# Gated linear attention with a rational MLP in fp32: the last 128 tokens leave as one piece, under another table of steps

## The chip, the cores and the metric

The kernel runs on one core of one Trainium2 chip. The metric is the time of one execution on the device, in microseconds (us); lower is better. The page of the profile and the trace come from one profiled execution, which has a time of its own beside those of the timed runs.

## What is computed

The inputs are q, k, v and alpha of 4 x 8 heads, 768 positions, 48 channels, and the weights of an MLP. Everything is fp32.

```python
state = zeros(B, H, D, D)                     # B=4, H=8, S=768, D=48
for t in range(S):
    state = alpha[:, :, t, :, None] * state + einsum('bhd,bhe->bhde', k[:, :, t], v[:, :, t])
    y[:, :, t] = einsum('bhd,bhde->bhe', q[:, :, t], state)
x = y.transpose(0, 2, 1, 3).reshape(B * S, H * D)   # 3072 x 384
h = x @ w_in                                        # 384 -> 2048
P = a[0] + a[1] * h + a[2] * h**2 + a[3] * h**3
Q = 1 + abs(b[0]) * abs(h) + abs(b[1]) * h**2
out = (P / (Q + 1e-6)) @ w_out                      # 2048 -> 384
```

## The kernel before

**Steps and their order.** The whole kernel is a list of 2813 steps, each a small function for one engine, added to a `Plan` with the steps that must come before it. `Plan.run` (L44) writes them out in the order of a table of numbers, `ORDER` (L72 to L139): each number is the index of a step, and its top bit says that the step's alternate engine is taken, where it has one. The engines' queues run in order, so the table settles what stands behind what on each engine, and which engine does a step that two can do. For a step on DVE that is marked `lock`, the next POOL step in the table waits until it has ended (L60 to L66).

**Attention.** 24 chunks of 128 tokens, named by g. Per chunk alpha is transposed on DVE (L454), k and q are transposed (L459), running products are made by a scan (L462) and a reciprocal (L471); k and q are scaled by them on POOL or DVE (L483, L486), the scores are copied by ACT (L525) and masked by POOL (L531), PE forms the products (L504, L537, L568, L586), and POOL and ACT carry totals and the state (L545, L547, L556, DVE L597). The output of a chunk, a piece of x, is copied out of PSUM by ACT and split into a high and a low part, the low part on DVE (L633, or for the first four chunks L626 on DVE or POOL).

**MLP.** 96 units of 128 x 512 elements of h, named by u: 16 slices of the 2048 columns for each super-block of 512 tokens; the first 8 are smaller, plain fp32 ones. A unit's input product on PE (L695, 9 matmuls of high and low parts) goes into one of three banks, so unit u waits until unit u - 3 has left its bank. Then ACT takes the absolute value (L750) and a linear part (L753), ACT or POOL makes the start of Q (L759 on ACT, L757 on POOL), POOL multiplies (L762), DVE makes P (L773, L777, L787), ACT adds and takes the reciprocal (L780, L783), DVE finishes (L790, L796: the step `g`), ACT rounds the result to its high part (L799: `gh`), POOL or DVE makes the low part (L803: `gl`), and PE multiplies with w_out (L714; L708 in the last super-block, where tokens stand on partitions).

**Weights.** They arrive as doubles and are put together to fp32 from their words: scaled (L270 on ACT or L272 on POOL: `join_scale`), shifted (L278 on DVE), their sign (L282) and the joining itself (L298 on DVE: `join`); the high part is rounded on ACT (L313) and the low part made on POOL (L318).

**A guard** reads alpha again in the second half (L849 on ACT), sums up (L859 on DVE, L862 on PE) and leaves a number (L865) that every engine loads at the end.

**The end.** The last super-block's output stands in four banks, one for each tile tt of 128 tokens x 384 columns. After the last unit's low part, PE adds the last products tile by tile (L723; `og` is the high part's, `ot` the low part's). Then `last_done` (L738) copies a tile out of PSUM, on ACT by an activation (L741), on DVE by a copy (L743), and `last_store` (L745) sends it to DRAM (L747). Tiles 0 and 2 are copied by DVE, tile 1 by ACT, and SP's queue issues their stores. Tile 3 is cut into two halves of 192 columns: the first is copied by DVE and stored by SP, the second copied by ACT and stored by ACT's own queue. The plan's code for this is at L1122 to L1133.

## Time and profile before

| | us |
|---|---|
| median of 3 runs | 529.98 |
| lowest, highest | 529.82, 531.18 |
| the profiled execution's own time | 531.47 |
| its span, first to last instruction | 529.4 |
| PE busy (share of the span) | 501.9 (95%) |
| DVE busy | 494.2 (93%) |
| ACT busy | 459.1 (87%) |
| POOL busy | 423.5 (80%) |

The profiled execution takes 2.07 us more than its span, which lie outside the instructions. The mean granted clock of TensorE is 0.988. A busy share is an average over stages: the first quarter of the span holds the attention's start and the weights, the middle runs both parts side by side, and the end holds the MLP alone. Units, chunks and tiles are told apart by the order of their instructions on an engine, since a row of the trace names only the line.

### The profile page before, as it was taken

To read this page: it belongs to the slowest core of one execution; us is meant where nothing else is said; L and a number is where in the kernel's file an instruction comes from. 1 tells how busy PE (TensorE), PEld (TensorE's weight loads), DVE (VectorE), ACT (ScalarE), POOL (GpSimd) and SP (SyncE) were. 2 spreads that over 40 slices of the span, in tenths; PEclk is the share of its full clock that TensorE was granted. 3 is DMA by queue.
4 is the path that set the end of the run, shared out by engine and by line. 5 is a ranking of instruction groups with operands and counts; after the bars stand their busy time and mean duration, and the time that the engine had idled before them with its cause. 6 is when DMAs were issued, how large, how long until landed. Compare 5 with 4: busy or idle time off the path is not lost.

```text
span 529.4 us, 13659 instructions
## 1 busy us (share of the span) xinstructions
PE 501.9 (95%) x5082; PEld 411.9 (78%) x5082; DVE 494.2 (93%) x773; ACT 459.1 (87%) x805; POOL 423.5 (80%) x421
## 2 busy tenths in 40 slices
PE   7865988987999999999999999999999999999996
PEld 7864866865778778778787887878888878888996
DVE  4899899999999999999999999999999999898885
ACT  4988999999999888888898898898898897997892
POOL 3447667999999998989898888889888887876782
PEclk9997998999999999999999999999999999999998
DMA  9899684465565454554546445351646201023001
GB/s 262 248 250 268 155 197 88 106 152 132 127 144 117 89 105 100 97 99 94 119 86 116 111 91 100 83 113 32 120 83 130 47 2 41 0 61 59 2 2 63
DMA packets 145656, 56.81 MB, mean 107 GB/s; under 512 B 133424, under 2 KB 138160, under 8 KB 145584
## 3 DMA queue, kind: packets, MB, share of 16 engines
q1 hardware_dynamic: 145440, 55.78, 46.4%
q8 instruction: 41, 0.67, 0.6%
q14 instruction: 31, 0.25, 0.2%
q10 hardware_dynamic: 144, 0.10, 0.1%
HBM read 47.98 MB, written 4.72 MB: 100 GB/s over the span
## 4 chain that ended last, share of the span: by engine, by line
PE 81%; ACT 6%; DVE 4%; SPq 4%; DMA 3%; issue 1%; POOL 1%; DVEq 0%; POOLq 0%
PE ps L695 34%; PE ps L714 28%; PE ps L708 6%; PE ps L586 4%; PE ps L681 2%; PE ps L504 2%; PE ps L568 2%; SPq L408 2%; PE ps L537 1%; DMA wi_words<-in_moe_w_in_dram 1%; ACT wo_words L282 1%; DMA wo_words<-in_moe_w_out_dram 1%; PE ps L668 1%; SPq L448 1%; SPq L401 1%
## 5 line engine op out<-in xcount | busy, mean ns | idle before, releaser
L695 PE MATMUL ps<-x,wi 128*128 128x512 f32 x792 | 204.4, 398 | 1.7 <-DVE t L796 1.7
L695 PEld LDWEIGHTS ps<-x,wi 128*128 128x128 f32 x792 | 146.5, 188 | 34.7 <-DVE t L796 2.7
L714 PE MATMUL ps<-gh_gl,wo 128*128 128x512 f32 x648 | 170.2, 399 | 0.2 <-ACT gh_gl L799 0.2
L714 PEld LDWEIGHTS ps<-gh_gl,wo 128*128 128x128 f32 x648 | 119.1, 188 | 27.2 <-ACT gh_gl L799 0.6
L762 POOL TENSOR_TENSOR qm<-qm,ah 128x512 f32<-128x512 f32 x96 | 124.2, 1294 | 14.8 <-ACT qm L759 5.9
L803 POOL TENSOR_TENSOR gh_gl<-t,gh_gl 128x512 fp32r<-128x512 f32 x83 | 108.6, 1309 | 16.3 <-ACT gh_gl L799 11.8
L753 ACT ACTIVATE t<-ps,coef 128x512 f32<-128x512 f32 x96 | 74.7, 778 | 6.9 <-PE ps L695 4.8
L787 DVE SCALAR_TENSOR_TENSOR t<-t,coef,ps 128x512 f32<-128x512 f32 x96 | 70.7, 737 | 6.5 <-ACT ps L783 5.1
L780 ACT ACTIVATE ps<-qm,one_eps 128x512 f32<-128x512 f32 x96 | 66.4, 691 | 11.5 <-DVE t L777 6.1
L750 ACT ACTIVATE ah<-ps 128x512 f32<-128x512 f32 x96 | 57.0, 594 | 20.6 <-PE ps L695 19.4
L777 DVE SCALAR_TENSOR_TENSOR t<-t,coef,ps 128x512 f32<-128x512 f32 x96 | 70.9, 739 | 1.0
L757 POOL TENSOR_SCALAR qm<-ah,bab 128x512 f32<-128x512 f32 x61 | 47.9, 786 | 28.6 <-ACT ah L750 16.8
L773 DVE TENSOR_TENSOR t<-t,ps 128x512 f32<-128x512 f32 x96 | 64.9, 677 | 4.6 <-ACT t L753 2.9
L796 DVE SCALAR_TENSOR_TENSOR t<-ps,t 128x512 f32<-128x512 f32 x96 | 65.6, 683 | 1.1
L790 DVE SCALAR_TENSOR_TENSOR ps<-qm,ps 128x512 f32<-128x512 f32 x96 | 65.9, 687 | 0.2
L783 ACT ACTIVATE ps<-ps 128x512 f32<-128x512 f32 x96 | 56.1, 585 | 2.0
L799 ACT ACTIVATE gh_gl<-t 128x512 fp32r<-128x512 f32 x88 | 55.1, 627 | 3.0 <-DVE t L796 2.8
L531 POOL TENSOR_SCALAR_AFFINE_SELECT tqk<-tqk 64x512 f32<-64x512 f32 x48 | 33.1, 690 | 13.9 <-ACT tqk L525 7.6
L486 POOL TENSOR_TENSOR tqk<-tqk,fp 128x512 f32<-128x512 f32 x22 | 28.9, 1312 | 8.9 <-DVE wi_words L298 7.7
L462 DVE TENSOR_TENSOR_SCAN tg<-ta,ps 128x528 f32<-128x528 f32 x24 | 29.7, 1242 | 6.6 <-ACT ta L444 6.5
L586 PEld LDWEIGHTS ps<-tqk,sv 128*32 128x32 f32 x1536 | 23.4, 112 | 15.1 <-POOL tqk L531 7.1
L483 POOL TENSOR_TENSOR tqk<-tqk,tg 128x512 f32<-128x512 f32 x23 | 30.4, 1322 | 5.6 <-ACT tqk L444 5.3
(112 smaller groups left out, 728.8 us busy)
## 6 DMA issues: line engine op xcount, KB each, us to landing
...
sv<-in_v_dram SPq DMA_DIRECT2D x48, 96.0 KB, 2.6
...
```

What stands on the lines that cost most here:

```text
L695: nc.tensor.matmul(h_of(u), w(key)[:, kt * FU + f % FU, :], x[:, kt, xp, :], start=(n == 0), stop=(n == len(todo) - 1),)
L714: nc.tensor.matmul(bank(O_BANKS[dt]), w(("o", f // FU))[:, f % FU, dt * P : (dt + 1) * P], g, start=(f == 0 and first_w), stop=(f == NF - ...
L750: nc.scalar.activation(buf(s, "ah", u), h_of(u), AF.Abs)
L753: nc.scalar.activation(buf(s, "t1", u), h_of(u), AF.Identity, bias=a2, scale=a3)
L762: nc.gpsimd.tensor_tensor(buf(s, "qm", u), buf(s, "qm", u), buf(s, "ah", u), op=ALU.mult)
L773: nc.vector.tensor_tensor(t, t, h_of(u), op=ALU.mult)
L777: nc.vector.scalar_tensor_tensor(t, t, a1, h_of(u), op0=ALU.add, op1=ALU.mult)
L780: nc.scalar.activation(h_of(u), buf(s, "qm", u), AF.Abs_reciprocal_sqrt, bias=one_eps)
L787: nc.vector.scalar_tensor_tensor(t, t, a0, h_of(u), op0=ALU.add, op1=ALU.mult)
L790: nc.vector.scalar_tensor_tensor(h_of(u), buf(s, "qm", u), 1.0 + 1e-6, h_of(u), op0=ALU.add, op1=ALU.mult)
L796: nc.vector.scalar_tensor_tensor(t, h_of(u), 2.0, t, op0=ALU.subtract, op1=ALU.mult, reverse0=True)
L803: eng.tensor_tensor(buf(s, "gl", u).rearrange("p a b -> p (a b)"), buf(s, "t1", u), gh, op=ALU.subtract)
```

## The change

Tile 3 is no longer cut. ACT copies all of its 128 x 384 elements and ACT's queue stores them; the other three tiles are as they were. That leaves 2811 steps instead of 2813: one copy and one store fewer.

```diff
-    def last_done(eng, tt, c0, c1):
-        o, x = parts[:, tt * DM + c0 : tt * DM + c1], bank(T_BANKS[tt], DM)[:, c0:c1]
+    def last_done(eng, tt):
+        o = parts[:, tt * DM : (tt + 1) * DM]
         if eng is nc.scalar:
-            eng.activation(o, x, AF.Copy)
+            eng.activation(o, bank(T_BANKS[tt], DM), AF.Copy)
         else:
-            eng.tensor_copy(o, x)
+            eng.tensor_copy(o, bank(T_BANKS[tt], DM))
-    def last_store(eng, tt, c0, c1):
+    def last_store(eng, tt):
         r = (NSUP - 1) * SUP + tt * P
-        eng.dma_start(out[r : r + P, c0:c1], parts[:, tt * DM + c0 : tt * DM + c1])
+        eng.dma_start(out[r : r + P, :], parts[:, tt * DM : (tt + 1) * DM])
...
-                    cut = DM // 2 if tt == PER - 1 else DM
-                    for c0 in range(0, DM, cut):
-                        part = (m, tt, c0) if c0 else (m, tt)
-                        act = c0 > 0 or tt == 1
-                        add(("wd", *part), "ACT" if act else "DVE", 0.5 if cut == DM else 0.33, last_done, (nc.scalar if act else nc.vector, tt, c0, c0 + cut), [("ot", tt)] + old, due=at + 3)
-                        add(("ws", *part), "ACT" if c0 else "SP", DMA, last_store, (nc.scalar if c0 else nc.sync, tt, c0, c0 + cut), [("wd", *part)], kb=0.55 * cut / DM)
+                    act, own = tt % 2, tt == PER - 1
+                    add(("wd", m, tt), "ACT" if act else "DVE", 0.5, last_done, (nc.scalar if act else nc.vector, tt), [("ot", tt)] + old, due=at + 3)
+                    add(("ws", m, tt), "ACT" if own else "SP", DMA, last_store, (nc.scalar if own else nc.sync, tt), [("wd", m, tt)], kb=0.55)
```

The table `ORDER` is replaced by another of 2811 numbers (two of its lines are enough to see that nothing can be read from them):

```diff
-    'c-jTQ1E3u`3;@t3X_~gPZQHhO+qS*k?fK2NZQHhO+xFi-XN*!Rx^gOtLN!)RQeLr&t;VUzDykZ<jGCubs3|I%TBxR~`D&t',
+    'c-jrsgQ6X}5&+Q5WG0iOwr$(CZQHin-5#IXwr$(CZQH(mZ~ep?qm=T>DORYWsOV~v8mD5ZXey?Pt&AG4mZ`C7o|>#ysJLp',
```

Forty-six steps go to the other one of their two engines. The start of Q goes to ACT 43 times (35 before) and to POOL 53 times (61), though at the start it goes to POOL for units 0, 1 and 10 and to ACT for units 2 and 9. The low part `gl` goes to DVE 8 times (5 before), six of them among the last ten units, where it was one. One `join_scale`, the fourth of w_in, moves from ACT to POOL (L272). The low part of x for chunk 1 moves from DVE to POOL (L626). One scaling of q, three score copies and five copies of totals change sides as well. The rest of the table keeps its broad sequence, with steps exchanged over a few places.

**POOL, early.** The stretch between the masking of chunk 1 (L531 on tqk_89) and that of chunk 2 (L531 on tqk_90). Before:

```order
L531 AFFINE_SELECT tqk_89<-tqk_89 64x8x64 x2
L62 MEMSET floor_s 128x1
L483 TENSOR_TENSOR tqk_90<-tqk_90,tg_86 128x512
L486 TENSOR_TENSOR tqk_88<-tqk_88,fp_85 128x512
L762 TENSOR_TENSOR qm_103<-qm_103,ah_98 128x512
L483 TENSOR_TENSOR tqk_88<-tqk_88,tg_87 128x512
L556 TENSOR_TENSOR sv_91<-st_s,tots_94 48x4x48
L556 TENSOR_TENSOR sv_91<-st_s,tg_86 48x4x48
L356 MEMSET raw_odd_82 128x48
L531 AFFINE_SELECT tqk_90<-tqk_90 64x8x64 x2
```

After, on the same engine at the same place:

```order
L483 TENSOR_TENSOR tqk_90<-tqk_90,tg_86 128x512
L626 TENSOR_TENSOR x_358<-x_whole,x_358 128x3x128
L757 TENSOR_SCALAR qm_103<-ah_98,bab 128x512
L272 TENSOR_SCALAR parts<-wi_words 128x768
L556 TENSOR_TENSOR sv_91<-st_s,tots_94 48x4x48
L556 TENSOR_TENSOR sv_91<-st_s,tg_86 48x4x48
L762 TENSOR_TENSOR qm_103<-qm_103,ah_98 128x512
L757 TENSOR_SCALAR qm_104<-ah_99,bab 128x512
L762 TENSOR_TENSOR qm_104<-qm_104,ah_99 128x512
L483 TENSOR_TENSOR tqk_88<-tqk_88,tg_87 128x512
L531 AFFINE_SELECT tqk_90<-tqk_90 64x8x64
```

The scaling of q for chunk 3 (L486 on tqk_88) now comes behind the masking of chunk 2; the low part of x for chunk 1, the start of Q for units 0 and 1, the scaling of a piece of w_in and the product of unit 1 have moved ahead of it.

**DVE, around the end of unit 12** (its L796 is the one on t_100; the L298 on parts and wo_words is the joining of the eighth piece of w_out). Before:

```order
L633 TENSOR_TENSOR x_1106<-ps,x_1106 128x3x128
L462 SCALAR_TENSOR_TENSOR tg_86<-ta_83,ps 128x528
L298 SCALAR_TENSOR_TENSOR parts<-parts,wo_words 128x768
L787 SCALAR_TENSOR_TENSOR t_100<-t_100,coef,ps 128x512
L773 TENSOR_TENSOR t_101<-t_101,ps 128x512
L790 SCALAR_TENSOR_TENSOR ps<-qm_103,ps 128x512
L777 SCALAR_TENSOR_TENSOR t_101<-t_101,coef,ps 128x512
L796 SCALAR_TENSOR_TENSOR t_100<-ps,t_100 128x512
L459 STREAM_TRANSPOSE tqk_90<-raw_qk_81 128x16x2x32
```

After:

```order
L462 SCALAR_TENSOR_TENSOR tg_86<-ta_83,ps 128x528
L796 SCALAR_TENSOR_TENSOR t_102<-ps,t_102 128x512
L787 SCALAR_TENSOR_TENSOR t_100<-t_100,coef,ps 128x512
L471 RECIPROCAL ta_83<-tg_86 128x4
L773 TENSOR_TENSOR t_101<-t_101,ps 128x512
L790 SCALAR_TENSOR_TENSOR ps<-qm_103,ps 128x512
L777 SCALAR_TENSOR_TENSOR t_101<-t_101,coef,ps 128x512
L796 SCALAR_TENSOR_TENSOR t_100<-ps,t_100 128x512
L298 SCALAR_TENSOR_TENSOR parts<-parts,wo_words 128x768
L459 STREAM_TRANSPOSE tqk_90<-raw_qk_81 128x16x2x32
```

The joining has moved from ahead of unit 12's last operations to behind them, and a reciprocal of 128 x 4 has come in.

**ACT, at the end** (t_102 is the last unit's). Before:

```order
L799 ACTIVATE gh_gl<-t_101 128x512
L799 ACTIVATE gh_gl<-t_102 128x512
L741 ACTIVATE parts<-ps 128x384
L741 ACTIVATE parts<-ps 128x192
L747 DMA out_dram<-parts 128x192
```

After:

```order
L799 ACTIVATE gh_gl<-t_101 128x512
L799 ACTIVATE gh_gl<-t_102 128x512
L849 ACTIVATE wr_78,beyond<-wr_78,lim 128x512
L741 ACTIVATE parts<-ps 128x384 x2
L747 DMA out_dram<-parts 128x384
```

The half copy and the half store have become whole ones, and the guard's last activation stands between the last unit's rounding and the first of ACT's copies. On DVE the copy of 128 x 192 is gone and the guard's sum (L859) has come in ahead of the two copies that stay; on SP the store of 128 x 192 is gone. On PE the last products of a tile (`og`, then `ot`) now follow each other tile by tile, where before `og` of the next tile came ahead of `ot` of the one before.

## Rows read from the trace of the kernel before

**Rows 1.** Busy time by stretch: us, then busy us (x instructions) by engine, PEclk, DMA, GB/s.

```profile
20.00:40.00 20.00, 15.03 (x287) 13.63 (x285) 18.54 (x27) 17.88 (x33) 8.93 (x10) 1.00 0.95 280
120.00:140.00 20.00, 17.28 (x193) 13.09 (x192) 19.82 (x31) 18.54 (x33) 19.16 (x18) 1.00 0.54 124
140.00:440.00 300.00, 300.00 (x3056) 239.85 (x3056) 293.57 (x466) 264.61 (x488) 266.09 (x257) 1.00 0.46 96
480.00:522.00 42.00, 42.00 (x216) 38.51 (x215) 36.30 (x56) 33.50 (x60) 31.08 (x28) 1.00 0.05 8
```

**Rows 2.** Waits of PE from 100 to 140 us: us in total, times, longest.

```profile
PE ps L568 <- ACT tqk L525: 1.6, 1, 1.6
PE ps L537 <- DVE x L633: 1.6, 1, 1.6
PE ps L695 <- DVE t L796: 1.1, 1, 1.1
```

**Rows 3.** Timeline of the end: start, us, engine, line, operation, idle before and its releaser.

```profile
521.96 0.69 DVE L803 TENSOR_TENSOR gh_gl<-t,gh_gl 128x512 fp32r<-128x512 f32 x1 [0.81 <-ACT gh_gl L799]
522.33 2.26 PE L723 MATMUL ps<-wo,gh_gl 128*128 128x384 f32 x12
523.93 0.49 ACT L741 ACTIVATE parts<-ps 128x384 f32<-128x384 f32 x1 [2.06 <-PE ps L723]
...
524.11 0.89 DVE L743 COPY parts<-ps 128x384 f32<-128x384 f32 x2
525.02 0.33 ACT L741 ACTIVATE parts<-ps 128x192 f32<-128x192 f32 x1 [0.60 <-DVE parts L743]
525.39 0.39 ACTq L747 DMA_DIRECT2D out_dram<-parts  x1
...
524.91 0.90 SPq L747 DMA_DIRECT2D out_dram<-parts  x2
```

**Rows 4.** DMA issues from 515 to 530 us: tiles, queue, count, KB each, us to landing.

```profile
out_dram<-parts SPq DMA_DIRECT2D x3, 192.0 KB, 2.0
out_dram<-parts ACTq DMA_DIRECT2D x1, 96.0 KB, 2.0
out_dram<-parts SPq DMA_DIRECT2D x1, 96.0 KB, 2.2
```

**Rows 5.** Timeline of DVE and of POOL from 122 to 130 us.

```profile
123.89 2.46 DVE L298 SCALAR_TENSOR_TENSOR parts<-parts,wo_words 128x768 uint32<-128x768 uint32 x1
...
128.78 0.68 DVE L796 SCALAR_TENSOR_TENSOR t<-ps,t 128x512 f32<-128x512 f32 x1
...
123.69 1.84 POOL L318 TENSOR_TENSOR wi<-wr,wi 128x768 fp32r<-128x768 f32 x1
```

**Rows 6.** DVE and ACT by line and tiles: count, busy us, mean ns, idle before.

```profile
L626 DVE TENSOR_TENSOR x<-x_whole,x 128x384 fp32r<-128x384 f32 x2 | 1.1, 550 | 0.4 <-ACT x L622 0.4
...
L298 DVE SCALAR_TENSOR_TENSOR wo_words<-wr,wo_words 128x768 uint32<-128x768 uint32 x2 | 1.9, 952 | 0.0
...
L759 ACT ACTIVATE qm<-ah,bab 128x512 f32<-128x512 f32 x35 | 28.5, 814 | 0.6 <-DVE ps L790 0.5
```

**Rows 7.** Timeline of DVE and of PE around 153 us (the L796 is unit 17's, the L695 unit 20's).

```profile
152.61 0.69 DVE L796 SCALAR_TENSOR_TENSOR t<-ps,t 128x512 f32<-128x512 f32 x1
...
153.71 0.73 PE L695 MATMUL ps<-x,wi 128*128 128x512 f32 x2
```

**Rows 8.** Timeline of POOL from 20 to 46 us.

```profile
36.01 1.27 POOL L486 TENSOR_TENSOR tqk<-tqk,fp 128x512 f32<-128x512 f32 x1 [7.67 <-DVE wi_words L298]
```

**Rows 9.** POOL by line and tiles, whole span.

```profile
L757 POOL TENSOR_SCALAR qm<-ah,bab 128x512 f32<-128x512 f32 x61 | 47.9, 786 | 28.6 <-ACT ah L750 16.8 <-DVE gh_gl L803 2.8 <-ACT t L753 2.1
...
L318 POOL TENSOR_TENSOR wi<-wr,wi 128x768 fp32r<-128x768 f32 x6 | 11.1, 1851 | 0.2
...
L626 POOL TENSOR_TENSOR x<-x_whole,x 128x384 fp32r<-128x384 f32 x2 | 2.0, 1016 | 1.7 <-DVE wo_words L278 1.7
```

**Rows 10.** Busy time by stretch, 100 to 180 us, columns as in rows 1.

```profile
100.00:180.00 80.00, 75.42 (x798) 58.98 (x797) 78.95 (x124) 75.67 (x128) 77.40 (x67) 1.00 0.54 125
```

More of the change, by code (lines that the diff above doesn't have):

```diff
@@ L133 @@
[L133 to L136 removed]
+    'c-jrsgQ6X}5&+Q5WG0iOwr$(CZQHin-5#IXwr$(CZQH(mZ~ep?qm=T>DORYWsOV~v8mD5ZXey?Pt&AG4mZ`C7o|>#ysJLp',
+    'mile5eg=)T<swS$aYPL$NR;meVhFYW+sKsivTB4Q))&;s@ckGFvdSG4^U#(K{RDbM+q<Z5<wMK1F(^Mbqi%HdVbz03)Wz{',
@@ new lines @@
+    'B?K=s3{YOOk@2I3aIUTxLe)MhmR)2Z}oyV7bD&QjZg&ZrE5-D(idRD*G^8iEN`MzvK9!{L};z0eaz1@M6Su7j|E8i701P@',
+    'JohsV!<G?okKTF11qyV<^^D+w~!}U+vH@bw2e&ztXRD2=3Hxg31Nv;RzLn6Y-=vtlsKy{Hc?xYpSUFrO&G0K@nJ0{n7hWi',
+    'oj?rua2m3SWq2T?{tO07`&+7>#_J(A5+=X2W^$1NX)LrV?}jd<p_M#N7a8irK+z!>3V7s4p0r$KmA!>QD5|BB{T&sDT<*c',
+    '<9q}vu8=%A+NGn?1+`l@QP)*56^-K29(_rbP@1OVLp2SfP<*Pcrek!9K@U_z)k)37SvUuCs;~N+o{cl`o+_zgQUY3ljZ`c',
+    'mI;ZC1Q<W%q5!O%(F*YTnB$SxeU~6?>-B5dVQmUqIs>Xq)s+oGOlF=YlQ{7Q_RdQlVLHl%CN=J{>3zd@6QwDmbGE>Ij!72',
@@ new lines @@
+    '`AqCC`GrJ^hpm)7D{wO_YTc_}NUru>wKx~R4)8)c``REXNB$Eu}zrEaOk*iJ3MeDqR1Q9acg)hcjXm7xN`pH&WOua;p>>a',
+    '4!0vQ(IAQ90_MDpEmOhr?A@RfK-1j)A2(P`y^=gS)AsG(;`O-l`bYre3NN^-;y?t*SsJs4}g<FDe)1rYiJRt-`)4pjuLhs',
+    '!IQ<-)a|rQt#DztV?xhB@R{9Xf;NI-S|&6pnBAbO40_bPQO%r`lE&gN>M{<O(WD#^<BMFaiA@EIG`I5z(I}BhI&(bYDXVb',
+    'A8JfBs0sB`9cUx|RZVH6+JqYVQcdbd{i!20qyB+`v>7doQVu?<0i<9ncA{+<Ogk`yniD}3*omRknYQ2{>OzC51?|D@*p<S',
+    'A_aZ|g6{O<A5Sm6YU?|0eFcOHQL%JIcBLjzZR7k8MXgZCi?vxU`s~!{^_F;VJNn>a~j-}`@oO%RiQZE`u$>9Jd35=jnl>i',
@@ L137 @@
+    'bg!G4He;ivl<ex;x3hx%oak$#pR<Cpu<ezqU$SNYX`oSWm<__cnVpX=B8d49fM;Me<&enaFYztwN^i~UZ&%YXAf{ARz!Z}',
+    '&U=ZokLx_51vOf589rzx@9IB$L{y',
 ]
```

113 lines of the change are left out of this document (50 added, 63 removed).

## The prediction

> **What bounds the kernel now.** I read the busy time by stretch first [rows 1]. From 140 to 440 us PE is busy for all of its 300.00 us, and from 480 to 522 us for all of its 42.00. No idle PE time can be taken out of these stretches. What a new order can save lies ahead of about 130 us and behind the last product; it can also open gaps where there are none, since DVE is busy 293.57 of the 300 us and so has little to spare.
>
> Next I read PE's waits from 100 to 140 us [rows 2]: three are left there, 1.6, 1.6 and 1.1 us, behind ACT's score copy, DVE's low part of x and DVE's last operation on unit 12. In the stretch from 120 to 140 us DVE is busy 19.82 of 20 us [rows 1], so the way to shorten these waits is less DVE work in front of them. The end I read from the timeline [rows 3]: PE's last 12 products run from 522.33 for 2.26, to 524.59, and everything behind that is copy, store and the loading of the guard's number, 529.4 - 524.6 = 4.8 us to the end of the span.
>
> **The end, part by part.** Before: DVE copies tiles 0 and 2, then its half of tile 3, and ends at 524.11 + 0.89 = 525.00. ACT's half starts only at 525.02, 0.60 us of waiting that the trace puts down to DVE's copy, takes 0.33 and lets ACT's store be issued at 525.39 [rows 3]. SP issues its last two stores from 524.91 for 0.90 us, so the very last is issued from about 524.91 + 0.45 = 525.4. It lands 2.2 us later, at 527.6; ACT's lands 2.0 later, at 527.4 [rows 4].
>
> After: ACT's whole copy costs 0.49 (tile 1's row) and depends on PE alone. It starts at about 524.64, a little after 524.59, ends at 525.13 and lets the store be issued about 0.04 later, as 525.35 to 525.39 was [rows 3], at 525.17. The store is 192 KB now, as three of SP's were, and those landed in 2.0 us, no later than the 96 KB ones [rows 4]: 527.2. The last landing moves from 527.6 to 527.2, **-0.4**. SP has one issue less (-0.45) and can go on to the end sooner by that. The two bounds are -0.5, where SP's own sequence sets the end, and 0, where the loading of the guard's number sets it: that load is issued by all engines behind the guard's result, which isn't earlier. The trace has no row that says which of the two; I take -0.4, since landing and issue both move by that much.
>
> The guard's activation behind the last rounding on ACT and its sum on DVE lie beside PE's twelve last products, 2.26 us long [rows 3], so I cost them at nothing. ACT has 2.06 us idle there. If that cover were gone, the first copy would be late by under 1 us, and it isn't the last one. The tile-by-tile order on PE costs no product more. It brings `ot` of tile 0 forward by one `og`, two of the twelve products or 2 x 0.19 = 0.38 us. That one needs the last low part, which DVE ends at 521.96 + 0.69 = 522.65; its new place is 522.33 + 0.38 = 522.71. So the slack there falls from about 0.4 to almost nothing; a DVE that is late by 0.5 us would then cost 0.5. DVE gets low parts of six among the last ten units and loses two just ahead of them, but has 42.00 - 36.30 = 5.7 us idle from 480 on [rows 1]. I cost this at 0, with +0.5 as its other end.
>
> **The start, part by part.** Two changes on DVE matter for the last waits. The low part of x for chunk 1, 0.55 us on DVE, goes to POOL, where it takes 1.02 [rows 6, 9]. And the joining of the eighth piece of w_out moves from ahead of unit 12's end to behind it; it took 2.46 us [rows 5], where the others of its kind take 0.95 [rows 6].
>
> How much of this reaches the end is read at the first place where PE is gap-free afterwards. Unit 20's input product starts at 153.71 and needs unit 17's L796, which ends at 152.61 + 0.69 = 153.30: a slack of 0.41 [rows 7]. PE is one packed sequence from there on, so the end moves by what this product moves. What stands on DVE ahead of unit 17 differs by the 0.55 alone (the joining is behind unit 12 now, but still ahead of unit 17). If DVE stays as full as it is, unit 20 can start at 153.30 - 0.55 = 152.75, which is **-0.96**; the waits of 1.6, 1.6 and 1.1 then shrink by this sum between them, the 0.41 of slack being given up. If the joining also takes its usual 0.95 in its new place, another 2.46 - 0.95 = 1.51 go, and the sum is -2.47. The other end is 0: where POOL or ACT takes DVE's place as the engine that these waits come from. I take -0.96, since the joining's new place has POOL beside it as full as its old one, 77.40 of 80 us [rows 10].
>
> The row on the joining deserves a second look. It started at 123.89, 0.2 us after a POOL subtraction of two tiles that ran from 123.69 to 125.53; taken from that end, the joining lasted 126.35 - 125.53 = 0.82, about its usual length [rows 5, 6]. The Trainium skill has a rule for it (SBUF — State Buffer, "SBUF: two separate sides"): a GpSimd instruction and a DVE instruction with two SBUF inputs share a port pair as an exclusive lock, and whoever starts first keeps the other out for its whole instruction. The trace agrees. By that rule the sum is -0.96 if the joining's new place finds such a POOL instruction just begun again, and -2.47 if it finds POOL at rest; nothing in the order of the two engines' queues settles which.
>
> On POOL the early stretch gets four instructions more ahead of chunk 2's masking: the low part of x, 1.02; two starts of Q, 2 x 0.79 = 1.57; and a scaling of 128 x 768 [rows 9]. POOL shows no row for this scaling; its bounds are 0.79 x 768/512 = 1.18 (the same kind of operation on 512 columns) and 1.85 (POOL's other operation on 768 columns, with two inputs) [rows 9]. I take 1.2, by the kind. The sum is 3.8, up to 4.4. What hides it: POOL waited 7.67 us at 36.01 with its scaling of q behind a joining on DVE [rows 8], and was busy 8.93 of 20 us [rows 1]. That wait is now behind chunk 2's masking, and the new work stands in its place. So I cost it at nothing. With the cover gone, up to 3.8 us of it come later. ACT loses one scaling and three starts of Q early, gets two back, and gets eight more in all, 0.81 us each [rows 6]. Most of them lie in the gap-free stretch, where ACT is busy 264.61 of 300 us [rows 1]. I cost them at nothing: 35 us of idle ACT time stand against 8 x 0.81 = 6.5.
>
> **The sum.** -0.96 - 0.4 = -1.36, rounded to -1.3 for the rounding of the ends. The profiled execution took 531.47 us, 2.07 of them outside the span of 529.4; it would take 530.2, with a span of 528.1. It stands 1.5 above the median of the runs, 529.98, so the median becomes 528.7.
>
> **Rivals.** (1) **Only the end changes**: POOL or ACT holds PE at the last waits instead of DVE, and -0.4 remains: 529.6. For it speaks POOL's share there, 77.40 of 80 us. Against it: two of the three waits name DVE [rows 2]. (2) **Faster**: the joining is free of POOL in its new place, -2.47 - 0.5: 527.0. For it speaks that most joinings took 0.95; against it, that unit 15 and the next units have waits of their own, which become the bound once those go. (3) **Slower**: POOL's new early work doesn't fit into the 7.67 us, because the instructions in it wait for their inputs in another order than they stand in. Then up to 3.8 us of work is pushed down POOL's queue, PE's waits for maskings and scalings ahead of 140 us grow, and the start brings a loss instead of -0.96. Between 100 and 180 us POOL has 80 - 77.40 = 2.6 us to catch up [rows 10]. If it can use all of that, 3.8 - 2.6 = 1.2 stay, and with -0.4 of the end the time is 529.98 + 0.8 = 530.8; if it can use none of it, 529.98 + 3.8 - 0.4 = 533.4; the middle is 532.1. It decides from the point where POOL reaches 100 us more than 2.6 us later than before. For it speaks how full POOL is there; against it, that 7.67 is twice 3.8. (4) **The change doesn't do what it says**: ACT's last copy waits for something other than PE, or the whole piece lands later than two halves; then the end gives 0 and the start alone -0.96: 529.0.
>
> **How the numbers follow.** The forecast, within 0.7 of 528.7, gets 0.45; rival 1 gets 0.17, rival 2 gets 0.15, rival 3 gets 0.18, rival 4 gets 0.05. A measurement can tell about 0.3% from no change, 1.6 us: faster means below 528.4, slower above 531.6. Below 528.4 lie rival 2 and nearly half of the forecast's own case, 0.15 + 0.2 = 0.35; above 531.6 lies most of rival 3, 0.15; the rest, 0.5, is within. The range leaves out the upper part of rival 3, some 0.16, and little of rival 2, whose 527.0 is the sum of the lower bounds: 526.9 to 531.2.
>
> **What would show it.** In the trace after: ACT's second copy at L741 with 128 x 384 elements, idle before it put down to PE, its store issued about 0.5 us behind the last product, and 4.4 us from the last product to the end of the span where it was 4.8. PE's waits between 100 and 140 us that sum to about 3.4 us instead of 4.4, the joining behind unit 12's L796, and unit 20's input product about 1 us earlier. No wait of PE after 155 us. Wrong would be: POOL's masking as the releaser of PE's waits ahead of 130 us, POOL's wait of 7.67 us still there with the new work behind it, a PE wait for DVE's L803 at the end, or a joining near 2.5 us again, which leaves the start at no more than -0.96.

## The result, and the profile after

The changed kernel took 532.98 us (median of 16 runs, 529.98 to 536.55), the kernel before 529.92 beside it (16 runs, 528.25 to 532.85): a ratio of 1.0062, 95% interval 1.0035 to 1.0088. It is slower by 0.6%, where 528.7 was forecast, and lies above the range of 526.9 to 531.2. The runs of the changed kernel come in two groups: eight of the 16 at 529.98 to 532.17, eight at 533.79 to 536.55. The profiled execution is one of the second: 536.37 us, its span 534.6.

**The end** did what was forecast. This is its timeline (start, us, engine, line, operation, idle before and its releaser), and below it the DMA issues from 515 to 536 us:

```profile
528.01 2.27 PE L723 MATMUL ps<-wo,gh_gl 128*128 128x384 f32 x12
...
529.33 1.39 SPq L747 DMA_DIRECT2D out_dram<-parts  x3
...
530.32 0.49 ACT L741 ACTIVATE parts<-ps 128x384 f32<-128x384 f32 x1 [0.56 <-PE ps L723]
...
530.84 0.38 ACTq L747 DMA_DIRECT2D out_dram<-parts  x1
```

```profile
out_dram<-parts SPq DMA_DIRECT2D x3, 192.0 KB, 1.9
out_dram<-parts ACTq DMA_DIRECT2D x1, 192.0 KB, 2.0
```

PE's last products end at 528.01 + 2.27 = 530.28. ACT's whole copy now waits for PE and no longer for DVE, where [rows 3] had 0.60 of idle behind L743. Its store goes out 0.56 behind the last product, lands in 2.0, and the span ends 534.6 - 530.3 = 4.3 us behind the product; before, [rows 3], it was 4.8.

**The start** lost time. PE's timeline around chunk 0's last products (L586):

```profile
14.11 2.84 PE L425 MATMUL ps<-ident,raw_second 128*128 128x128 f32 x24
16.88 1.11 PE L586 MATMUL ps<-tqk,sv 128*32 128x64 f32 x61
21.06 0.43 PE L586 MATMUL ps<-tqk,sv 128*32 128x64 f32 x3 [3.07 <-issue]
```

Of 64 products of one kind 61 run, and the last three come after 3.07 us in which PE waited for nothing that the profile shows ("issue"). The kernel before has no such stop; its 64 run in one piece:

```profile
17.75 1.10 PE L586 MATMUL ps<-tqk,sv 128*32 128x64 f32 x64 [0.63 <-DVE st_s L601]
```

Unit 0's input product comes at 26.84, where it came at 23.86 before. PE's longest wait from 0 to 60 us, and all of its waits from 100 to 140 (us in total, times, longest):

```profile
PE ps L586 <- POOL lim L62: 6.1, 1, 6.1
...
PE ps L586 <- DVE sv L595: 2.2, 1, 2.2
PE ps L695 <- DVE t L796: 1.2, 1, 1.2
PE ps L504 <- DVE fp L474: 0.7, 1, 0.7
PE ps L504 <- ACT kt L540: 0.3, 1, 0.3
```

The last four answer to [rows 2]: 4.4 us there (with one of 0.2 that isn't shown there), 4.4 here, with other names. The wait of 6.1 is chunk 2's, behind POOL's masking (the row names L62, a small fill right behind the mask); before it was 4.2. The stretches that answer to [rows 1], columns as there:

```profile
20.00:40.00 20.00, 16.96 (x255) 15.05 (x254) 15.52 (x23) 16.39 (x32) 10.70 (x9) 0.83 1.03 280
...
120.00:140.00 20.00, 17.83 (x249) 13.88 (x248) 19.48 (x33) 18.74 (x31) 17.82 (x17) 0.91 0.54 120
140.00:440.00 300.00, 298.46 (x2988) 237.96 (x2987) 292.19 (x465) 272.67 (x498) 259.28 (x247) 1.00 0.45 95
```

The granted clock is 0.83 behind the stop and 0.91 behind 120 us, and the middle has 1.5 us of idle PE, two waits of L695 behind DVE's L796, where it had none. Following one step through both traces, the changed kernel is 0.9 us ahead at chunk 0's L586, then behind by 3.0 at unit 0, 4.8 at chunk 2, 3.3 at unit 10, 3.9 at unit 20 and 5.7 at the first of the last twelve products.

### The profile page after: what moved, and what is told of

It reads as the page before. It is cut to its first block, busy times and chain, and to the rows that moved or that the text cites. A ratio compares the mean times of both kernels' runs of the same rounds, so it can differ in the third digit from the quotient of the medians.

```text
span 534.6 us, 13656 instructions
## 1 busy us (share of the span) xinstructions
PE 506.0 (95%) x5082; PEld 414.5 (78%) x5082; DVE 497.0 (93%) x775; ACT 464.7 (87%) x810; POOL 422.3 (79%) x413
## 4 chain that ended last, share of the span: by engine, by line
PE 54%; SPq 12%; DVE 9%; ACT 9%; DMA 8%; POOL 4%; issue 3%; DVEq 0%; POOLq 0%; ACTq 0%
PE ps L695 22%; PE ps L714 18%; SPq L401 9%; PE ps L708 6%; PE ps L586 3%; DMA raw_a<-in_alpha_dram 2%; DMA wi_words<-in_moe_w_in_dram 2%; DMA wo_words<-in_moe_w_out_dram 1%; DVE t L796 1%; DVE t L777 1%; ACT wo_words L282 1%; PE ps L681 1%; PE ps L504 1%; PE ps L568 1%; DVE ps L790 1%
## 5 line engine op out<-in xcount | busy, mean ns | idle before, releaser
L695 PE MATMUL ps<-x,wi 128*128 128x512 f32 x792 | 201.8, 396 | 4.6 <-DVE t L796 4.5
L695 PEld LDWEIGHTS ps<-x,wi 128*128 128x128 f32 x792 | 146.5, 188 | 39.3 <-DVE t L796 7.0
L714 PE MATMUL ps<-gh_gl,wo 128*128 128x512 f32 x648 | 173.2, 402 | 0.0
L762 POOL TENSOR_TENSOR qm<-qm,ah 128x512 f32<-128x512 f32 x96 | 125.8, 1311 | 28.8 <-ACT qm L759 18.2
L803 POOL TENSOR_TENSOR gh_gl<-t,gh_gl 128x512 fp32r<-128x512 f32 x80 | 104.3, 1306 | 17.8 <-ACT gh_gl L799 13.2
L796 DVE SCALAR_TENSOR_TENSOR t<-ps,t 128x512 f32<-128x512 f32 x96 | 65.4, 681 | 1.0
L757 POOL TENSOR_SCALAR qm<-ah,bab 128x512 f32<-128x512 f32 x53 | 45.2, 853 | 18.9 <-ACT ah L750 10.6
L531 POOL TENSOR_SCALAR_AFFINE_SELECT tqk<-tqk 64x512 f32<-64x512 f32 x48 | 32.6, 680 | 10.8 <-ACT tqk L525 8.8
L483 POOL TENSOR_TENSOR tqk<-tqk,tg 128x512 f32<-128x512 f32 x23 | 30.1, 1307 | 13.4 <-ACT tqk L444 7.8
L586 PEld LDWEIGHTS ps<-tqk,sv 128*32 128x32 f32 x1536 | 24.4, 115 | 20.0 <-issue 7.0
L586 PE MATMUL ps<-tqk,sv 128*32 128x64 f32 x1536 | 28.8, 229 | 11.5 <-POOL lim L62 6.1
```

The lines of the kernel that those rows point to most:

```text
L586: nc.tensor.matmul(y[r : r + 32, o : o + CH], w[:, w0 : w0 + 32], tqk[g % NQ][:, int(j == c), a, toks(c)], start=r not in begun, stop=True ...
L695: nc.tensor.matmul(h_of(u), w(key)[:, kt * FU + f % FU, :], x[:, kt, xp, :], start=(n == 0), stop=(n == len(todo) - 1),)
L714: nc.tensor.matmul(bank(O_BANKS[dt]), w(("o", f // FU))[:, f % FU, dt * P : (dt + 1) * P], g, start=(f == 0 and first_w), stop=(f == NF - ...
L762: nc.gpsimd.tensor_tensor(buf(s, "qm", u), buf(s, "qm", u), buf(s, "ah", u), op=ALU.mult)
L796: nc.vector.scalar_tensor_tensor(t, h_of(u), 2.0, t, op0=ALU.subtract, op1=ALU.mult, reverse0=True)
L803: eng.tensor_tensor(buf(s, "gl", u).rearrange("p a b -> p (a b)"), buf(s, "t1", u), gh, op=ALU.subtract)
```

## The experiments

Three theories were tried: **fetch**, that the changed order of SP's loads delays something that PE's stop waits for; **POOL**, that its new early work pushes chunk 2's masking back; **order**, that the rest of the new table has its own waits in 30 to 130 us. In some of the kernels the lines stand two lower (L584 for L586, L745 for L747).

### The same kernel twice

> The kernel after once more, unchanged, for a second trace and more times beside the same runs of before. If the stop of PE at chunk 0's last products is a race between the fetch of its instructions and the loads, its length differs from the 3.07 us of the first trace, and the start of unit 3's input product and the total move with it one to one; the times spread over 530 to 536 again. If it is a fixed cost of the order, it is 3.1 us again and the times are as far from before in each execution.

532.18 against 529.06, 1.0067 [1.0036, 1.0098], 12 runs from 529.39 to 536.80. Its profiled execution was one of the lower group, 529.39, with the stop at the same instruction:

```profile
16.01 1.10 PE L586 MATMUL ps<-tqk,sv 128*32 128x64 f32 x61
18.32 0.30 PE L586 MATMUL ps<-tqk,sv 128*32 128x64 f32 x3 [1.21 <-issue]
```

So the place is no chance, 61 products and then the stop; its length differs from execution to execution. The two are 7.0 us apart. At chunk 0's L586 it is 0.9, at unit 0 it is 4.4 (26.84 against 22.45): the stop itself makes 1.9 of that, and the rest comes with the granted clock, 0.83 against 1.00 from 20 to 40 us.

This trace is not behind the one of before but ahead of it: unit 20's input product comes at 152.30, where it came at 153.71, and the span is 527.7 against 529.4. That looks like the forecast come true, and isn't: the trace of before is of an execution of 531.47, above the median, and in two other traces of its table (e1_tail and e5_tail_order, below) unit 20 comes at 152.10 and 151.54. Measured from chunk 0's L586 to unit 20, the table of before takes 136.0, 134.1 and 133.8 us; the new one 140.7 in after, 136.3 here, and 137.3 in a trace without the stop (e10_wi1_late, below).

### Where the stop comes from

SP's loads up to 19 us differ in order. Before (this L258 is the third piece of w_in, 768 KB by the page, not the 384 KB that the expectations below give it; L448 is chunk 1's v, 96 KB each):

```profile
13.45 2.34 SPq L448 DMA_DIRECT2D sv<-in_v_dram  x2
...
17.93 0.44 SPq L258 DMA_DIRECT2D wi_words<-in_moe_w_in_dram  x1
```

After:

```profile
12.81 0.43 SPq L258 DMA_DIRECT2D wi_words<-in_moe_w_in_dram  x1
13.29 2.82 SPq L448 DMA_DIRECT2D sv<-in_v_dram  x2
```

Among the DMA queues there is one of the kind instruction that moves blocks of 0.67 MB / 41 = 16 KB. Here is its row for the whole span of after; then the queue of the loads from 12.0 to 18.6 us, where the instruction queue moves nothing; then the first block that it moves since 12 us, in the 1.2 us behind (queue, kind: packets, MB, share of the 16 engines):

```profile
q8 instruction: 41, 0.67, 0.5%
...
q1 hardware_dynamic: 2366, 1.92, 89.8%
...
q8 instruction: 1, 0.02, 5.8%
```

In the kernel before that block moved between 14.2 and 15.4, though PE was 0.9 us later in its program. The loads' share alone is not the reason: from 12.0 to 14.2 us it is 122% in before and 108% in after (the share counts overlapping packets). That the blocks are PE's fits their number: PE has 5082 products and as many weight loads, 10164 instructions, or 248 for each of the 41 blocks; no other engine has over 810. And in the runs the first block's end and PE's next product go together:

| run | block moved | PE goes on | from block's end | stop |
|---|---|---|---|---|
| after | 18.61 to 19.72 | 21.06 | 1.34 | 3.07 |
| a0_after | 15.97 to 16.97 | 18.32 | 1.35 | 1.21 |
| e3_front_after | 17.53 to 18.49 | 19.93 | 1.44 | 1.58 |
| e4_wi2_late | 16.72 to 17.68 | 19.12 | 1.44 | 0.85 |
| e9_wi3_early | 15.92 to 16.88 | 18.33 | 1.45 | 1.03 |
| e7_pool_back | 16.88 to 17.85 | 19.09 | 1.24 | 0.75 |
| before | 14.20 to 15.39 | | | none |
| e10_wi1_late | 15.41 to 16.37 | | | none |

PE goes on 1.2 to 1.5 us after the block has come, whatever the size of the stop. What counts is when PE gets to its 61st product: in before the block's end lies 3.4 us ahead of that product's end, in e10_wi1_late 1.7, and PE doesn't stop; in e4_wi2_late it lies only 0.6 ahead, in after 1.7 behind. In e8_after_loads_before (below) the block ends at 17.81, later than in three of the six with a stop, and PE doesn't stop, since it gets to that product only at 21.5. e12_km6_early and e13_masks_early, with the loads of e10_wi1_late, have no stop either. When PE asked for the block, the trace doesn't show. The Trainium skill (DMA: Bandwidth & Descriptors, "Queues, rings and completion order") says that each DMA engine takes the queue rows in turn, one packet of each. By that rule alone a block that has been asked for waits for the packet in hand and not for all the loads that are queued; here it comes 4.4 us later in after than in before (1.8 in a0_after), so the rule doesn't account for the size, unless the request itself was late. No run settles which.

The first trial moves that one load back:

```diff
 L228 DMA coef<-in_moe_b_dram 128x2
-L258 DMA wi_words<-in_moe_w_in_dram 128x3x512
 L448 DMA sv_92<-in_v_dram 64x8x48 x2
+L258 DMA wi_words<-in_moe_w_in_dram 128x3x512
```

> The kernel after with one load moved in SP's queue: the third piece of w_in (384 KB in 12.81 us there) goes behind the two pieces of v for chunk 1. Theory A1: PE's gap of 3.07 us is the fetch of its next instructions, which is queued behind this load; then the gap is gone or under 0.5 us, unit 0's input product is back from 26.8 to about 24 us, and the time is 530 to 530.5. Rival A2: POOL's added work ahead of chunk 2's masking sets the time of chunk 2's products (48.97 us) by itself; then these stay at 48 us or later and the time stays at 532.5 to 533.

531.14, 1.0036 [1.0017, 1.0056], 8 runs from 530.35 to 532.73: no time lies in the upper group, the stop is 0.85 where under 0.5 was looked for, and some 0.4% over before remains. The same move the other way, the load put ahead of L448 in the kernel before:

> The kernel before with one load moved in SP's queue: the third piece of w_in goes ahead of the two pieces of v for chunk 1, from two places behind them. Theory A1 (the fetch of PE's instructions is queued behind this load): PE gets a stop that the trace puts down to nothing else, 1 to 3 us long near 18 us, and the time rises by 1 to 3 us, to 530 to 532. Rival: the load alone does nothing, 529 to 529.5, and the stop needs the rest of the order of after.

530.35, 1.0005 [0.9987, 1.0023]. Here it is the second block that is late (27.58 to 28.66, before 21.85 to 22.85), and the stop appears in a kernel that had none:

```profile
27.63 0.32 PE L586 MATMUL ps<-tqk,sv 128*32 128x64 f32 x8
30.04 1.55 PE L586 MATMUL ps<-tqk,sv 128*32 128x64 f32 x56 [2.09 <-issue]
```

PE goes on 1.38 behind the block's end. It lies largely beside the 4.2 us that chunk 2 waits anyway, and the last products start only 1.25 us later than in the trace of before; the median doesn't show it. So the order of the loads makes the stop, though the rise of 1 to 3 us in the time that was looked for isn't there; what a stop costs depends on where it falls.

Four more orders of the loads. In e10_wi1_late the second and third pieces of w_in both stand behind chunk 1's v:

```diff
 L408 DMA raw_second<-in_k_dram 128x8x96
-L258 DMA wi_words<-in_moe_w_in_dram 128x3x512
 L408 DMA raw_second<-in_q_dram 128x8x96
 L227 DMA coef<-in_moe_a_dram 128x4
 L228 DMA coef<-in_moe_b_dram 128x2
-L258 DMA wi_words<-in_moe_w_in_dram 128x3x512
 L448 DMA sv_92<-in_v_dram 64x8x48 x2
+L258 DMA wi_words<-in_moe_w_in_dram 128x3x512 x2
```

In e9_wi3_early the fourth comes forward to the third:

```diff
-L258 DMA wi_words<-in_moe_w_in_dram 128x3x512
+L258 DMA wi_words<-in_moe_w_in_dram 128x3x512 x2
 L448 DMA sv_92<-in_v_dram 64x8x48 x2
 L261 DMA wo_words<-in_moe_w_out_dram 128x2x768
 L401 DMA raw_a_80<-in_alpha_dram 32x4x96 x2
-L258 DMA wi_words<-in_moe_w_in_dram 128x3x512
```

e8_after_loads_before has the first 17 loads in before's order, and e11_v_first these with chunk 0's v in front of the pieces of w_in and of chunk 1; the place of v in the two:

```diff
-L448 DMA sv_91<-in_v_dram 64x8x48 x2
+L408 DMA raw_second<-in_alpha_dram 128x8x96
 L258 DMA wi_words<-in_moe_w_in_dram 128x3x512 x2
-L408 DMA raw_second<-in_alpha_dram 128x8x96
+L448 DMA sv_91<-in_v_dram 64x8x48 x2
 L408 DMA raw_second<-in_k_dram 128x8x96
```
(- is e11_v_first, + e8_after_loads_before.)

> The kernel after with two loads moved in SP's queue, the second and the third piece of w_in, both behind the two pieces of v for chunk 1. Theory A1: fewer bytes are queued when PE asks for its instructions near 13 us, so the stop at chunk 0's last products is under 0.5 us (0.8 with the third piece alone moved), no execution is above 533, and the median is 530 to 530.5. The second piece itself is needed for unit 1's input product; if it is late, PE waits there instead and the gain is lost.

> The suspected cost made larger: the kernel after with the fourth piece of w_in (another 384 KB) also ahead of the two pieces of v for chunk 1. Theory A1: PE's stop at chunk 0's last products grows to 3 to 6 us, and the median rises to 534 to 537. Rival: the stop stays between 1 and 3 us, since the fetch waits only for what was issued ahead of it; then the time moves only as far as chunk 1's v comes later.

> The kernel after with its first 17 loads in the order that they have in before (one of a set of four pieces of alpha aside), nothing else. Theory A1: PE's second block of instructions comes in right when it is asked for, near 14 us, the stop at chunk 0's last products is under 0.3 us, and the executions above 533 are gone. If the rest of the table of after gains what I forecast (1 us at the start, 0.45 at the end), the time is 528 to 528.5; if the rest gains nothing, 529; if the rest costs something too (rival B), 530 to 531.

> The kernel after with its first 17 loads in a third order: both pieces of v for chunk 0, which its PE order needs first, then the first two pieces of w_in together, then chunk 1's alpha, k, q and v, and the third piece of w_in behind all of them as in before. Theory A1: no stop of PE (under 0.3 us) and no wait for v (2.7 us in the run with the load order of before); the median is 528.5 to 529.5, level with before or under it, which would show that the rest of the table loses nothing. Rival B: with the stop gone it stays at 530.5 or more, and the rest of the table costs the difference.

| run | time | ratio | stop | instead |
|---|---|---|---|---|
| e10_wi1_late | 531.42 | 1.0057 [1.0036, 1.0078] | none | |
| e9_wi3_early | 533.30 | 1.0065 [1.0031, 1.0100] | 1.03 | |
| e8_after_loads_before | 533.31 | 1.0061 [1.0037, 1.0085] | none | PE waits 2.7 for v |
| e11_v_first | 532.63 | 1.0061 [1.0042, 1.0081] | none | PE waits 1.5 for the raw alpha of chunk 1 |

More bulk ahead (e9) did not make the stop longer in its one trace, a miss; as two traces of after differ by 1.86, this doesn't price the bytes. And e8 shows why the order can't simply be put back, since the new order of PE takes v first. The waits of these two runs, PE from 12 to 26 us:

```profile
PE ps L568 <- DMA sv<-in_v_dram: 2.7, 1, 2.7
...
PE ps L425 <- DMA raw_second<-in_alpha_dram: 1.5, 1, 1.5
```

With e10 the stop is out of the way in its trace (an execution of 531.52), and the kernel is still 0.57% slower; e8 and e11, without a stop but each with a new wait, miss the 528 to 529.5 that was looked for too. So the stop is not the whole loss, and its share isn't settled: e4 has 1.0036 and e10 1.0057, after 1.0062 and 1.0067, and the intervals overlap. Nor is the upper group of times shown to be the stop's alone: two of e10's eight times, 534.15 and 534.35, lie in it.

### The end by itself

e1_tail is the table of before with ACT's whole copy and store; the last products stay in before's order. e5_tail_order has after's order of them too. The edit that parts e1_tail (-) from e5_tail_order (+), PE's last steps by tile:

```diff
-og0 og1 ot0 og2 ot1 og3 ot2 ot3
+og0 ot0 og1 ot1 og2 ot2 og3 ot3
```

> The table of before (its two half steps of the last tile dropped) with the new end alone. All theories: the last product ends where it did in the kernel before, and the span ends 4.3 us behind it instead of 4.8; the median is 0.4 us under that of before, about 529.5. If it is not under it, the gain at the end seen in the trace after (4.32 us instead of 4.81) belongs to that execution and not to the change.

> The table of before with the new end, and the last products, copies and stores in the order of after (tile by tile), nothing else. Theory: the gain at the end comes from this order, which spreads the stores: 4.35 us from the last product to the end of the span, against 5.09 in the run with the old order and the same copies, and against 4.81 before; the median is 0.4 to 0.5 under that of before. Rival: 5.0 us again, then something else in the table of after spreads them.

e1_tail took 529.97, 1.0017 [1.0001, 1.0033]; e5_tail_order 529.33, 1.0002 [0.9985, 1.0019]. Neither is a gain in the times. In the traces they differ. e1_tail (the last products, SP's third store, ACT's), then ACT's issue, then the same of e5_tail_order:

```profile
520.65 2.26 PE L721 MATMUL ps<-wo,gh_gl 128*128 128x384 f32 x12
...
523.22 0.40 SPq L745 DMA_DIRECT2D out_dram<-parts  x1
...
523.47 0.38 ACTq L745 DMA_DIRECT2D out_dram<-parts  x1
```

```profile
out_dram<-parts ACTq DMA_DIRECT2D x1, 192.0 KB, 2.6
```

```profile
520.10 2.40 PE L723 MATMUL ps<-wo,gh_gl 128*128 128x384 f32 x12
...
522.59 0.33 SPq L747 DMA_DIRECT2D out_dram<-parts  x1
...
523.06 0.38 ACTq L747 DMA_DIRECT2D out_dram<-parts  x1
```

```profile
out_dram<-parts ACTq DMA_DIRECT2D x1, 192.0 KB, 2.0
```

In both, ACT's store is issued 0.56 behind the last product. In e1_tail SP's third store went out at 523.22, 0.25 us ahead of ACT's, and ACT's landed in 2.6; span minus last product is 528.0 - 522.9 = 5.1, worse than the 4.8 of before. In e5_tail_order SP's third left 0.47 ahead of ACT's, ACT's landed in 2.0, and the end is 526.8 - 522.5 = 4.3. So in these traces the whole copy gives nothing by itself; with the order of PE that spreads the stores it gives the half microsecond. What that order gives with the two halves wasn't run.

The table was equal up to the end in before, e1_tail and e5_tail_order, yet from 100 us on e1_tail's trace is 1.6 us ahead of before's and e5_tail_order's 2.2. They part between chunk 2's and unit 10's first products (44 to 99 us), where the stretches at a lower granted clock lie in other places: from 40 to 60 us it is 0.83 in before, 0.77 in e1_tail, 0.78 in e5_tail_order, and from 80 to 100 us 0.91, 1.00 and 1.00. Differences of some 2 us between two single traces of this kernel are therefore not evidence.

### Halves of the table

e2_front_before takes before's order up to the first step of unit 8 and after's from there; e3_front_after the reverse. Both have the new end.

> The table of before up to the first step of unit 8 (381 steps), from there the table of after, and the new end. Theory A: the loss lies in the first 50 us, where PE stands still for 3.07 us within chunk 0's last products, waiting for nothing but its own instructions, and again 6.14 us behind POOL; then this kernel loses nothing there and runs at about 529.5. Rival B: the loss lies in the later part, where ACT makes more of the starts of Q and PE waits 1.5 us after 140 us; then it stays at about 531 to 533.

> The other half: the table of after up to the first step of unit 8 (376 steps), from there the table of before, and the new end. Theory A: the loss is in it, 532.5 to 533. Rival B: it runs at about 529.5 to 530.

533.77, 1.0077 [1.0048, 1.0105], and 536.74, 1.0157 [1.0118, 1.0195]. Neither fits either theory: e2 is no faster than after, and e3 is slower than either whole. Probably the seam costs more than what was looked for; the halves don't price each other and settle nothing.

### POOL's early work

POOL's rows in the trace of after, from 36 us, and two of DVE's beside them:

```profile
36.91 3.16 POOL L272 TENSOR_SCALAR parts<-wi_words 128x768 f32<-128x768 f32 x1
...
41.52 1.86 POOL L762 TENSOR_TENSOR qm<-qm,ah 128x512 f32<-128x512 f32 x1
...
42.18 2.08 DVE L284 TENSOR_SCALAR wo_words<-wo_words 128x768 uint16<-128x768 uint16 x1
...
45.56 1.62 DVE L278 TENSOR_SCALAR wi_words<-wi_words 128x768 uint32<-128x768 uint32 x1
```

The scaling that was bounded by 1.18 and 1.85 took 3.16. Nine other traces have it on POOL: 3.13 or 3.14 in eight, 3.25 in e9_wi3_early. In all ten it began while a DVE operation was running, and from that one's end on it took 2.3 us more. In after that was a joining, L298, from 36.38 to 37.74. In e9_wi3_early it was L284, to 35.31, and DVE's L278 then ran inside the scaling at its usual length:

```profile
34.31 3.25 POOL L272 TENSOR_SCALAR parts<-wi_words 128x768 f32<-128x768 f32 x1
...
36.34 0.55 DVE L278 TENSOR_SCALAR wo_words<-wo_words 128x768 uint32<-128x768 uint32 x1
```

So some 0.8 us of it (1.0 in e9_wi3_early) can be waiting for DVE; the 2.3 that are left, with other DVE work beside it, look like the scaling's own length. No run has it alone.

Elsewhere the two engines do stretch each other by turns. DVE's L278 on w_in takes 0.56 on the mean before and 1.62 here, L284 1.07 to 1.15 on the mean before and 2.08 here, both beside POOL's L762; one L278 on w_out took 1.62 before too, beside POOL's L483. L284 at 42.18 began inside POOL's L762, which ended at 43.38, and ended 0.9 behind that. The Trainium skill (SBUF — State Buffer, "SBUF: two separate sides") says that the lock which the prediction named holds also against DVE operations in a two-port mode, which need no second input. The trace agrees beside L762 and L483, since L278 and L284 have one input each; it doesn't show whether they ran in such a mode. Beside L272 it doesn't agree: L284 ran inside it in 1.12 (after), L278 in 0.55.

In e7_pool_back, built on e4_wi2_late, the scaling and units 0's and 1's start of Q go back to ACT, chunk 1's low part of x back to DVE, and unit 1's product behind the masks. On POOL:

```diff
-L626 TENSOR_TENSOR x_358<-x_whole,x_358 128x3x128
-L757 TENSOR_SCALAR qm_103<-ah_98,bab 128x512
-L272 TENSOR_SCALAR parts<-wi_words 128x768
 L556 TENSOR_TENSOR sv_91<-st_s,tots_94 48x4x48
 L556 TENSOR_TENSOR sv_91<-st_s,tg_86 48x4x48
 L762 TENSOR_TENSOR qm_103<-qm_103,ah_98 128x512
-L757 TENSOR_SCALAR qm_104<-ah_99,bab 128x512
```

In e13_masks_early, built on e10_wi1_late, unit 1's two steps go behind chunk 2's masks:

```diff
-L757 TENSOR_SCALAR qm_104<-ah_99,bab 128x512
-L762 TENSOR_TENSOR qm_104<-qm_104,ah_99 128x512
 L483 TENSOR_TENSOR tqk_88<-tqk_88,tg_87 128x512
 L531 AFFINE_SELECT tqk_90<-tqk_90 64x8x64
 L62 MEMSET lim 128x1
 L531 AFFINE_SELECT tqk_90<-tqk_90 64x8x64
+L757 TENSOR_SCALAR qm_104<-ah_99,bab 128x512
+L762 TENSOR_TENSOR qm_104<-qm_104,ah_99 128x512
```

> The run with the late third piece of w_in (531.1), and besides it the early work taken off POOL again: the scaling of a piece of w_in and the starts of Q for units 0 and 1 on ACT, the low part of x for chunk 1 on DVE, unit 1's product on POOL behind chunk 2's masking. Theory P (POOL's work costs the chunk): from chunk 1's last products to chunk 2's it takes 16.8 us as in before, not 17.6, and the total falls by about 0.8, to 530.3. Rival: these 0.8 us are made up before 100 us, and the total stays at 531.

> The run without the stop (531.4), and on POOL the start of Q and the product of unit 1 behind chunk 2's masking, as before. Rival P: POOL's masking sets chunk 2's last products; then the masking comes 2 to 3 us earlier, the wait of 6.2 us falls to 4 or less, and the median falls by 1 or more, to 530.4 or less. Theory C: DVE's copy of chunk 2's state at 43.9 us and unit 0's last DVE operation at 45.9 are as late as the masking, so unit 3's input product stays at 46.5 to 46.9 and the median stays at 531 to 531.5.

534.37, 1.0086 [1.0063, 1.0109], and 533.51, 1.0064 [1.0034, 1.0095]: no gain, and e7_pool_back is slower than e4_wi2_late, on which it is built (1.0036 [1.0017, 1.0056]). In both the masks come earlier (38.5 to 41.3 and 41.4 to 44.0, where e10_wi1_late has 44.3 to 45.7), and PE waits just the same. Chunk 2's L586, first of e7_pool_back, then of e13_masks_early:

```profile
47.56 1.94 PE L586 MATMUL ps<-tqk,sv 128*32 128x64 f32 x64 [7.05 <-DVE sv L597]
...
44.76 1.94 PE L586 MATMUL ps<-tqk,sv 128*32 128x64 f32 x64 [5.80 <-DVE sv L597]
```

The releaser is now DVE's L597, an operation on chunk 2's state (in the tile sv), ahead of which DVE was busy without a break from 36 us on in both traces. In a0_after this wait ends at 44.66, with e10_wi1_late at 44.99, before at 44.17. In after POOL's first mask ends at 48.92 and L597 at 48.60, so the two arrive together; taking the work off POOL puts it on ACT and DVE, which are as full.

### The new wait at chunk 6

On DVE the new table puts the joining's shift (L278) and the subtraction for unit 10 (L803) ahead of chunk 6's copy L595. In a0_after:

```profile
115.00 1.01 DVE L278 TENSOR_SCALAR wo_words<-wo_words 128x768 uint32<-128x768 uint32 x1
115.93 1.25 DVE L803 TENSOR_TENSOR gh_gl<-t,gh_gl 128x512 fp32r<-128x512 f32 x1
117.11 0.73 DVE L595 COPY sv<-ps 48x192 f32<-48x192 f32 x2
...
117.98 1.10 PE L586 MATMUL ps<-tqk,sv 128*32 128x64 f32 x64 [2.19 <-DVE sv L595]
```

Before, the copy came at 115.65, ahead of these two. e12_km6_early is e10_wi1_late with the copy put back:

```diff
+L595 COPY sv_91<-ps 48x4x48 x2
 L278 TENSOR_SCALAR wo_words<-wo_words 128x768
 L803 TENSOR_TENSOR gh_gl<-t_101,gh_gl 128x512
-L595 COPY sv_91<-ps 48x4x48 x2
```

> The run without the stop (second and third piece of w_in late, 531.4), and on DVE the copy of chunk 6's state ahead of a shift on w_out and unit 10's low part again, as in before. Theory C: PE's wait of 2.1 us at chunk 6's last products goes, the granted clock doesn't fall behind it, unit 15's input product comes 1.2 to 2.2 us earlier, and the median is 529.2 to 530.2. Rival P: the loss lies at chunk 2; then unit 15 is set by DVE all the same and the median stays at 531 to 531.5.

531.59, 1.0034 [1.0012, 1.0057], where e10_wi1_late had 1.0057 [1.0036, 1.0078]: the intervals overlap, and the 529.2 to 530.2 that was looked for didn't come. Its trace says more. Unit 15 comes at 127.48, 2.7 us ahead of e10_wi1_late, as hoped; but then

```profile
117.33 1.10 PE L586 MATMUL ps<-tqk,sv 128*32 128x64 f32 x64 [1.62 <-POOL tqk L531]
...
135.84 2.10 PE L695 MATMUL ps<-x,wi 128*128 128x512 f32 x8 [0.90 <-DVE x L633]
...
154.29 2.34 PE L695 MATMUL ps<-x,wi 128*128 128x512 f32 x9 [0.90 <-DVE t L796]
```

chunk 6's wait only falls from 2.13 to 1.62, now behind POOL; two waits of 0.90 behind DVE are new, and unit 20 comes at 154.29, where e10_wi1_late had it at 154.26. The gain is given back within 27 us. In that stretch DVE isn't full, it waits for loads of k, and these two are its only waits from 124 to 155 us:

```profile
129.23 1.25 DVE L459 STREAM_TRANSPOSE tqk<-raw_qk 128x1024 f32<-128x1024 f32 x1 [1.13 <-DMA raw_qk<-in_k_dram]
...
146.07 1.25 DVE L459 STREAM_TRANSPOSE tqk<-raw_odd 128x1024 f32<-128x1024 f32 x1 [1.17 <-DMA raw_odd<-in_k_dram]
```

SP issues the first of these loads from 126.64, where e10_wi1_late has it from 125.58: an alpha load ahead of it in SP's queue waited 1.3 us for DVE. So PE came earlier and SP's loads later, and DVE, waiting for them, gave back most of what PE had gained.

## Why the prediction was wrong, point by point

**The end, -0.4: the size was right, the cause was not.** The span ends 4.3 us behind the last product, as forecast (4.4). But the prediction took it from ACT's whole copy and costed PE's new order at nothing. e1_tail has the copy without the order and ends at 5.1; e5_tail_order has both and ends at 4.3. The row that was trusted, 2.0 us for 192 KB [rows 4], doesn't hold in e1_tail, where the store is issued 0.25 us behind another. Rival 4, that the whole piece lands later, is what e1_tail shows in its one trace. In the times the gain doesn't show: 1.0002 [0.9985, 1.0019].

**What was left out: SP's queue.** The prediction read the change on PE, ACT, DVE and POOL, and never what was moved past what among the loads. There lies the largest single new loss of the trace: PE's instruction block late by 4.4 us and a stop of 3.07 (1.8 and 1.21 in the other trace). That the load order makes the stop is shown from both sides (e10_wi1_late takes it away, e4_wi2_late leaves 0.85, e6_before_wi2_early brings one into the kernel before); why the block is late stays open, and so does the stop's share of the 0.6%. No rival named it, and the rows that were chosen had nothing of SP's first 20 us; that the loads change places could be read from the two orders.

**The start, -0.96: the step that failed is "If DVE stays as full as it is, unit 20 can start at 152.75".** It came at 157.59 in after, and at 154.26 with the stop out of the way (e10_wi1_late). That it came at 152.30 in a0_after is luck of the execution, since two traces of the old table have it as early or earlier. It is true that 0.55 us left DVE. But the order decides which wait PE meets, and in the changed table chunk 6's copy stands behind two operations it used to precede. The waits of 4.4 us in 100 to 140 us stayed 4.4 and changed their names (3.9 in a0_after). Nor does their sum set the time: in e1_tail and e5_tail_order, with the old table there, it is 2.8, and from unit 10 to unit 20 they take 55.1 and 55.2 us as before does (55.1). e12_km6_early shows how it goes on: chunk 6's copy put right brings unit 15 forward by 2.7, then DVE waits for SP's loads of k and PE for DVE.

**POOL's early work, costed at nothing: wrong, but not by much that could be undone.** The low part of x, the scaling and the two starts of Q took 1.33 + 3.16 + 1.49 + 1.36 = 7.3 us in after instead of 3.8, the scaling alone 3.16 instead of 1.2; and the sum had left out unit 1's product, which moved ahead of the masking too, 1.95 us, against 1.27 of the scaling of q that moved behind it. PE's wait at chunk 2 rose from 4.2 to 6.1 with POOL's masking as its releaser, the very sign that was named as wrong. Rival 3 with its middle of 532.1 comes nearest to the time. Its mechanism alone falls: with masks early (e7_pool_back, e13_masks_early) DVE's L597 holds PE as long.

**The joining: the better case came, and brought nothing.** Behind unit 12's end it took

```profile
131.91 1.46 DVE L298 SCALAR_TENSOR_TENSOR parts<-parts,wo_words 128x768 uint32<-128x768 uint32 x1
...
127.25 0.95 DVE L298 SCALAR_TENSOR_TENSOR parts<-parts,wo_words 128x768 uint32<-128x768 uint32 x1
```

1.46 in after and 0.95 in a0_after, in place of 2.46 [rows 5]. Rival 2 counted on just this and on -2.47 for it. The 1.0 to 1.5 us saved on DVE are in the same stretch in which PE's waits stayed at 4.4 and 3.9.

**What is left without the stop.** e10_wi1_late and e5_tail_order have the same end. Between their traces e10_wi1_late falls behind by 1.4 us up to chunk 3, by 0.2 more up to unit 10, 1.2 up to unit 15, and 0.2 in the rest, 3.0 in all; the medians, each against its own runs of before, say 1.0057 against 1.0002. The first part builds up from chunk 0, where e10_wi1_late is still 0.7 ahead, to chunk 3, the second around chunk 6. Part of both is the clock: at unit 8, e10_wi1_late and a0_after have

```profile
84.64 3.85 PE L695 MATMUL ps<-x,wi 128*128 128x512 f32 x9 [1.99 <-DVE t L796]
...
84.10 2.34 PE L695 MATMUL ps<-x,wi 128*128 128x512 f32 x9 [1.80 <-DVE t L796]
```

the same nine products behind nearly the same wait, in 3.85 us and in 2.34. The granted clock over just these stretches is 0.56 and 1.00: for most of the 3.85 PE ran at 1.2 GHz instead of 2.4. It comes in some executions and not in others. How much of the remaining 0.3 to 0.6% is waits and how much clock stays open; one trace of each kernel can't tell it.

**The range** missed because its upper end, 531.2, left out most of rival 3 and knew nothing of the stop. No version here beats the kernel before; e5_tail_order is level with it.
